# A fused attention and long-convolution kernel on one core: another prologue, and the order of the fill

## The chip, the cores and the metric

The kernel runs on one core of a Trainium2 chip. The metric is device time of one execution in microseconds (us), the median of several runs. A core has five engines that run their own instruction streams and meet at semaphores: TensorE (PE, matrix products into PSUM; its weight loads are counted apart as PEld), VectorE (DVE), ScalarE (ACT, here above all the exponential), GpSimd (POOL) and SyncE (SP, here only issuing DMAs). Several engines issue DMAs on queues of their own.

## What is computed

Two independent parts, side by side in the output of 2048 rows and 2 x 512 columns. Part A is attention with 32 heads of 16 columns that share one k and one v. Part B is a short causal convolution of k (4 taps) times v, then a causal convolution over all 2048 positions per channel, a skip term and a gate.

```python
q = (x @ wq).reshape(B, S, H, Dh).transpose(0, 2, 1, 3)      # S = 2048, D = 512, H = 32, Dh = 16
k, v = x @ wk, x @ wv                                        # one head of 16 for all
p = softmax(einsum("bhqd,bkd->bhqk", q, k) * Dh ** -0.5)
a = einsum("bhqk,bkd->bhqd", p, v).transpose(0, 2, 1, 3).reshape(B, S, D) @ wo

k_shift = sum(k_pad[:, t:t+S] * shift_k[:, 3-t] for t in range(4))
kv = k_shift * v
y = irfft(rfft(kv, 2S) * rfft(ssm_k, 2S))[:S] + kv * ssm_D
b = q * y
out = concatenate([a, b], axis=-1)
```

## The kernel before

**Attention in tiles.** Queries are cut in four quarters of 512, heads in groups of four; one such pair is a stack, 32 in all (`NQ`). A stack is 16 blocks of 128 keys times two, 32 tiles. A tile is: scores (`keys`, L937: eight products, 49 rows of the contraction) into one of two PSUM buffers, one exponential on ACT over 128x1024 (`exp`, L949), and products with v (`pv`, L973) that sum over the keys. The 49 rows are q's high part, its low part, one row with a bound on the score, and the high part again; so the exponential cannot overflow and no running maximum is needed. That row holds the norm bound |q| times max |k|, computed by PE from |q| and the maxima of k (`bound`, L709). High and low parts are two float16 tiles whose sum is the float32 value; a product of such numbers is three float16 products.

**Stacks go through DRAM.** Queries and bounds of four heads are written to the DRAM tile `qd`, and `stack` reads 49 rows per head back into the tile `st`. That puts the rows on the partitions on which the scores want them. Also the very first stack goes this way, except its bound row.

**The prologue** (`prologue`, `load`, `x_turn`) comes before the first tile. x arrives in four quarters of 1 MB. PE transposes each 128x128 block (L576), ACT makes the high part while it copies out of PSUM (L589), DVE the low part (L592). The first query group of the first quarter is multiplied out (L770, twelve products), clipped (L683), split and sent. Then k and v of all positions (`kv`, L601), their maxima over the positions (`km`, L610), the largest of them by head column (`k_max`, L645 to L651), k's rows in place (`kv_rows`, L617; `k_cut`, `k_rows`), the bound row (`first_bound`, `first_rows`, L722 and L729), and the first scores. Between these stand products on a tile of zeros whose result nobody reads (`warm`, L567).

**The fill.** `attend` writes the program tile by tile. Everything that is not scores, exponential and PV products is given by generator threads (`_Fill`): the other queries (`rest_of_q`), the convolution as Fourier transforms by products and butterflies (`conv_pe`, `conv_short`, `conv_dve`), the output projection (`wo_part`), the last keys of four stacks whose exponential DVE computes (`own`), and the way of x's quarters 2 and 3 to DRAM and back (`spill`). A thread yields how many products it wants, and a DVE cost; `turn` gives room on PE by the constants SLOT, SCORES, PV, UNIT and on DVE by a credit of RATE per tile. The order of the threads in `body` is their priority; `hurry` raises one that is near a due time. `after` holds a thread until another has set a mark. One PSUM buffer pair (tag f) of two holds the sums of PV, the other is left to the fill; each fill group starts when DVE has read the group before it.

Of the kernel before, what the change touches and what calls it, by code (L numbers as in the profile page):

```python
# [109 lines left out]
class _Emit:  # L110
# [75 lines left out]
    def dft16(self, c, first, second, sign):  # L186
# [39 lines left out]
        self.places = (f1, f2)  # L226
# [210 lines left out]
    def backward(self, blk, cx, places):  # L437
# [3 lines left out]
        g1, g2 = places  # L441
# [11 lines left out]
        yield WAIT, 5  # L453
# [21 lines left out]
    def conv_pe(self):  # L475
# [13 lines left out]
        yield from self.after(("y", 0))  # L489
        yield from self.backward(0, *self.sp["y", 0])  # L490
        yield from self.short(1)
        yield from self.after(("y", 1))
        yield from self.backward(1, *self.sp["y", 1])
# [23 lines left out]
    def conv_dve(self):  # L517
        nat = [0, 1, 2, 3]
        for blk, order in enumerate((("cx", "ch"), ("ch", "cx"))):
            for n in order:  # L520
                yield from self.after((n, blk))
                yield from self.dft16(self.sp[n, blk], nat, nat, -1)
            f1, f2 = self.places
            cx, ch = self.sp["cx", blk], self.sp["ch", blk]
            yield from self.product(cx, ch)
            self.seen.add(("p", blk))
            yield from self.dft16(cx, f2, f1, 1)
            self.sp["y", blk] = cx, self.places
            self.seen.add(("y", blk))


    def load(self):
# [6 lines left out]
        nc.scalar.dma_start(wkv[:, :, DH:32], I["A_wv"].rearrange("(k p) e -> p k e", p=P))  # L539
        self.msk = self.c.tile([P, 295], F32, name="msk")  # L540
        nc.scalar.dma_start(self.msk, I["msk"])
        xa = w.tile([P, 4, D], F32, tag="sp", bufs=1, name="xa")
# [5 lines left out]
        wqf = [w.tile([P, 4, P], F32, tag="s2", bufs=S2, name=self.nm("wqf")) for g in range(4)]  # L548
        self.wq = [w.tile([P, 2, 4, P], F16, tag="wq", bufs=4, name=self.nm("wq")) for g in range(4)]
        for c in range(4):  # L550
            for i in range(2):
                nc.sync.dma_start(self.xin[c][i], xr[c][:, 2 * i : 2 * i + 2, :])
            if c == 0:
                nc.sync.dma_start(wqf[0], wq[:, :, 0:P])
        for g in range(1, 4):
# [5 lines left out]
        self.parts(nc.gpsimd, self.wkv[:, 0], self.wkv[:, 1], wkv, WS)  # L561
        self.wqf = wqf
# [6 lines left out]
    def x_turn(self, c, b, between=lambda: None, cut=None):  # L569

        nc = self.nc

        def turn(dp, rows):
            for e in range(2):
                for i in rows:
                    nc.tensor.transpose(  # L576
                        b[dp][:, e, i * P : (i + 1) * P],
                        self.xin[c][i // 2][:, i % 2, (2 * dp + e) * P : (2 * dp + e + 1) * P],
                        self.ident,
                    )  # L580

        for rows in (range(2), range(2, 4)):
            for dp in range(2):
                turn(dp, rows)
            if rows.start == 0:
                between()
        for dp in range(2):
            hi, lo = (self.xT[c][:, i, 2 * dp : 2 * dp + 2, :] for i in range(2))
            nc.scalar.mul(hi, b[dp], XS)  # L589
            if cut is not None and dp == 0:  # L590
                self.q_hi(0, 0, cut)
            nc.vector.scalar_tensor_tensor(lo, b[dp], XS, hi, ALU.mult, ALU.subtract)  # L592
        if cut is not None:
            self.q_abs(0, 0, cut)

    def kv(self, b):

        order = [(i, j, dk) for dp in range(2) for i, j in ((0, 0), (1, 0), (0, 1)) for dk in (2 * dp, 2 * dp + 1)]
        for x in order:
            for c in range(4):  # L600
                self.nc.tensor.matmul(  # L601
                    b[32 * c : 32 * c + 32, :],
                    self.wkv[:, x[0], x[2], :],
                    self.xT[c][:, x[1], x[2], :],
                    start=x == order[0],
                    stop=x == order[-1],
                )
        kv = self.w.tile([P, 512], F32, tag="p", bufs=PB, name="kv")
        self.km = self.c.tile([P, 1], F32, name="km")
        self.nc.vector.tensor_reduce(self.km, b, AX.X, ALU.max, apply_absolute_value=True)  # L610
        self.nc.scalar.copy(kv, b)
        return kv

    def kv_rows(self, kv, c, b):

        r = slice(32 * c, 32 * c + 32)
        self.nc.tensor.matmul(b, self.msk[r, 163:291], kv[r, :], start=True, stop=True)  # L617

    def k_cut(self, b, a=0, n=512):
        cut = self.w.tile([P, n], F32, tag="s2", bufs=S2, name=self.nm("kc"))  # L620
        lim = lambda i: self.msk[:, 160 + i : 161 + i]
        self.nc.vector.tensor_scalar(cut, b[:, a : a + n], lim(0), lim(1), ALU.min, ALU.max)
        h16 = self.w.tile([P, n], F16, tag="gn", bufs=3, name=self.nm("kh"))
        return cut, h16

    def k_rows(self, c, cut, h16, a=0, n=512):

        ks = self.kst[:, c * 512 + a : c * 512 + a + n]
        self.nc.vector.scalar_tensor_tensor(ks, h16, self.msk[:, 162:163], cut, ALU.mult, ALU.add)

    def v_turn(self, kv, b):

        nc = self.nc
        for t in range(4):
            nc.tensor.transpose(b[:, t * P : (t + 1) * P], kv[:, t * P : (t + 1) * P], self.ident)
        bv = b.rearrange("p (t c m) -> p t c m", t=4, c=4)
        vx = self.vx.rearrange("p (c t) m -> p t c m", t=4)[:, :, :, 0:DH]
# [827 lines left out]
```

## Time and profile before

| what | value |
|---|---|
| median of three runs | 1005.63 us (1001.79 to 1005.63) |
| the profiled execution | 1004.58 us |
| its span, first to last instruction | 1002.3 us |
| mean granted TensorE clock | 0.993 |
| first exponential starts | 32.40 us |
| exponentials | 1016, busy 938.1 us |
| DMA | 83.12 MB |

The span is the time between the first and the last instruction in the trace; the execution's own time is taken from outside and 2.3 us longer. Busy time is the union of an engine's instructions, so 95% on ACT and 94% on PE do not say which of the two is the limit: that is read from what ended the idle time of each. The granted clock is the share of full speed that the throttle let TensorE have. A tile's row in the trace has the line of its helper, so all scores are L937 whatever the stack.

### The profile page before, as it was taken

What the parts mean: (1) busy time and instruction counts of PE and PEld (TensorE: products, weight loads), DVE (VectorE), ACT (ScalarE), POOL (GpSimd) and SP (SyncE); (2) the same over time, 40 slices, a digit from 0 to 9 for tenths busy, and PEclk for the clock granted to TensorE, in tenths of its full rate; (3) what the DMA queues carried; (4) which work ended last, traced back from release to release, by engine and by line L of the source; (5) the groups of instructions that cost most, each with busy time, mean ns of one, the idle gap of its engine ahead of it and who ended that gap; (6) DMA issues with size and microseconds to landing.
All of it is one profiled execution on the core that took longest, in us unless ns stands there. A gap on an engine that the chain in (4) does not pass through costs nothing.

```text
span 1002.3 us, 51255 instructions
## 1 busy us (share of the span) xinstructions
PE 940.9 (94%) x23463; PEld 459.4 (46%) x23463; DVE 746.3 (74%) x964; ACT 950.6 (95%) x1032; POOL 172.3 (17%) x305
## 2 busy tenths in 40 slices
PE   7999999999999999999989999999889989989996
PEld 4344444444544444444444544544334444444453
DVE  4637966888627988989888678599998827667753
ACT  4699999999999999999999999999999999999995
POOL 1542211410004000100054254000000033111000
PEclk9899999999999999999999999999999999999999
DMA  6262432423213211322143344111111133121101
GB/s 222 82 187 83 135 115 90 110 86 96 74 55 92 69 44 37 95 86 65 44 141 120 95 138 124 56 36 41 55 44 44 43 121 103 59 80 43 46 13 47
DMA packets 69461, 83.12 MB, mean 83 GB/s; under 512 B 20816, under 2 KB 58550, under 8 KB 69238
## 3 DMA queue, kind: packets, MB, share of 16 engines
q1 hardware_dynamic: 47430, 43.78, 13.8%
q0 software_dynamic: 20320, 35.46, 11.9%
q8 instruction: 185, 3.03, 1.3%
q10 hardware_dynamic: 1488, 0.54, 0.2%
q14 instruction: 38, 0.31, 0.1%
HBM read 54.66 MB, written 25.03 MB: 80 GB/s over the span
## 4 chain that ended last, share of the span: by engine, by line
PE 51%; ACT 26%; DVE 14%; issue 6%; DMA 2%; SPq 0%; POOL 0%; ACTq 0%; DVEq 0%; POOLq 0%
ACT p L949 26%; PE f L973 24%; PE s L937 14%; PE f L250 11%; DVE own L1036 3%; DVE sp L169 1%; DVE ao L982 1%; DMA xb<-in_A_x 1%; DVE ao L983 1%; DVE sp L290 1%; DVE sp L435 0%; PE f L617 0%; DMA qd<-qp 0%; DMA ff<-in_ff 0%; PE f L576 0%
## 5 line engine op out<-in xcount | busy, mean ns | idle before, releaser
L949 ACT ACTIVATE p<-s 128x1024 f32<-128x1024 f32 x1016 | 938.1, 1068 | 19.2 <-PE s L937 17.1
L973 PE MATMUL f<-p,vx 64*32 64x512 f32 (+1 forms) x8880 | 551.8, 554 | 2.2 <-DVE cut L683 1.1
L937 PE MATMUL s<-st,kst 49*32 49x512 f16 x8128 | 428.8, 381 | 33.2 <-ACT p L949 29.2
L937 PEld LDWEIGHTS <-kst 49*32 49x32 f16 x8192 | 200.2, 89 | 399.5 <-issue 353.2
L973 PEld LDWEIGHTS f<-p,vx 64*32 64x32 f32 x8880 | 175.4, 106 | 30.5 <-issue 3.7
L169 DVE TENSOR_TENSOR sp<-sp 128x1024 f32<-128x1024 f32 x96 | 111.1, 1215 | 0.0
L290 DVE COPY sp<-f 128x1024 f32<-128x1024 f32 x32 | 39.1, 1223 | 64.1 <-PE f L250 64.1
L295 POOL DMA_DIRECT2D ff<-in_ff x64 | 34.5, 545 | 277.8 <-ACT p L949 276.1
L982 DVE COPY ao<-f 128x512 f32<-128x512 f32 (+1 forms) x33 | 22.2, 674 | 55.2 <-PE f L973 55.1
L250 PE MATMUL f<-wo,o 64*32 64x512 f16 x1440 | 57.0, 375 | 1.7 <-DVE cut L683 0.9
L169 DVE TENSOR_TENSOR sp<-sp,sp 128x1024 f32<-128x1024 f32 x48 | 56.1, 1217 | 0.3
L250 PE MATMUL f<-xT,wq 64*32 64x512 f16 x1344 | 53.4, 375 | 1.8 <-DVE gm L733 1.2
L295 POOL DMA_DIRECT2D fi<-in_fi x32 | 17.8, 560 | 180.3 <-ACT p L949 180.3
L250 PE MATMUL f<-a,ff 64*32 64x256 f32 x1024 | 42.4, 378 | 1.1 <-DVE a L407 0.6
L250 PE MATMUL f<-hT,ff 64*32 64x256 f32 x1024 | 40.8, 377 | 1.3 <-DVE sp L290 1.2
L467 DVE TENSOR_TENSOR r<-f,q 128x512 f32<-128x512 f32 x16 | 11.0, 689 | 41.2 <-PE f L250 41.2
L250 PE MATMUL f<-sp,fi 64*32 64x256 f32 x1024 | 40.4, 376 | 0.9 <-DVE r L467 0.9
L469 POOL DMA_DIRECT2D out<-r x32 | 17.8, 560 | 124.7 <-DVE r L467 114.1
L405 DVE TENSOR_TENSOR a<-a,t 128x512 f32<-128x512 f32 x48 | 33.2, 692 | 1.6
L396 DVE TENSOR_TENSOR t<-kk,tpb 128x512 f32<-128x512 f32 (+1 forms) x50 | 33.0, 663 | 0.9 <-DMA qd<-qp 0.9
L323 POOL DMA_DIRECT2D hin<-in_B_ssm_k x32 | 21.1, 665 | 64.5 <-ACT p L949 63.1
L250 PEld LDWEIGHTS <-o 64*32 64x32 f16 x1440 | 22.6, 93 | 16.2 <-DVE cut L683 1.8
(166 smaller groups left out, 732.3 us busy)
## 6 DMA issues: line engine op xcount, KB each, us to landing
ff<-in_ff POOLq DMA_DIRECT2D x64, 128.0 KB, 2.9
od<-ao SPq DMA_DIRECT2D x60, 128.0 KB
qd<-qp SPq DMA_DIRECT2D x48, 128.0 KB
st<-qd SPq DMA_DIRECT2D x62, 98.0 KB
kk<-in_B_k POOLq DMA_DIRECT2D x32, 128.0 KB, 2.8
v<-in_B_v POOLq DMA_DIRECT2D x32, 128.0 KB, 3.4
hin<-in_B_ssm_k POOLq DMA_DIRECT2D x32, 128.0 KB, 5.5
fi<-in_fi POOLq DMA_DIRECT2D x32, 128.0 KB, 3.3
```

Of the source, the lines that this page charges most:

```text
L169: v.tensor_tensor(part(out), part(a), part(b), op)
L250: y = self.nc.tensor.matmul(out[j : j + 32, cols], w[r, j : j + 32], x[r], start=half == m == 0, stop=half == 1 and m == k - 1,)
L290: self.nc.vector.tensor_copy(out, self.both.rearrange("p i (q n) -> p i q n", q=2))
L295: self.paced(self.nc.gpsimd.dma_start(t[:, i], self.I[n][:, 2 * m2 + i]))
L323: self.paced(nc.gpsimd.dma_start(dst, src))
L396: nc.vector.tensor_tensor(out[:, n], kk[:, x], tap(i, n.stop - n.start), ALU.mult)
L405: nc.vector.tensor_tensor(a, a, t, ALU.add)
L937: self.nc.tensor.matmul(s[j : j + 32, e, :], self.kst[rows, k * P + j : k * P + j + 32], self.st[n][rows, a, cols], start=True, stop=True,)
L949: self.exps[u % 4] = self.nc.scalar.activation(self.pt[u], s, AF.Exp, scale=LN2 * DH**-0.5 / SC / SC)
L973: nc.tensor.matmul(self.acc[e][32 * j : 32 * j + 32, m], vx[rows, :], y, start=k == 0, stop=stop)
L982: nc.vector.tensor_copy(a, self.acc[0][:, m])
L1036: v.scalar_tensor_tensor(g, g if i < 4 else y, c[i], y if i else x.bitcast(BF16), ALU.add, ALU.mult)
```

## The change

**Prologue.** x's transposes, high parts and low parts are cut in pieces (`x_turn`, `x_hi`, `x_lo`) and written out in one list, with the twelve query products in between and no products on zeros but the first ten. The low part of x's last quarter isn't made there: ACT copies the transposed values from PSUM to the tile `xa`, and fill makes it later. The first stack's query rows are put in place on chip: `sel`, a matrix of zeros and ones made by POOL from the identity, is multiplied with the split queries, and the bound is summed into the same PSUM by the weights `wbn`. The bound uses a maximum of k that comes from the product of the high parts alone (`kv_max`), with -1.02 for the scale. k's first 512 columns come in two halves from weights `wkx` that hold wk at the row places (`k_first`). The high parts of three query weights stay on POOL, the low parts go to DVE, as fill. v's weights are loaded on SP's queue and split later.

**First stack.** Exact k and v (`kv`), the other k rows in halves of 256 (`k_chunk`), v's transposes (`v_turn`), the missing low part, the exact maximum and a check that the first bound held (into `gm`) are the start of `rest_of_q`. The PV products of the first stack start at tile 7 in place of 3, by a table in `plan`; its first four exponentials go to a buffer of their own.

**Later stacks.** The queries of the second quarter wait for the transforms of the first channel half (`cx`, `ch`), those of the last quarter for `cx` of the second; the inverse transform's thread starts its loads at a mark `soon`, 28 steps into the last butterflies, in place of at their end; the third stack's load is issued at tile 22 of the second. The last store's second half is issued by ACT in place of SP.

On ACT in the prologue, from the conversions of the third quarter of x to the first exponential. Names: `xT` high parts of x, `wq` query weights, `qp` and `qa` split and absolute queries. Before:

```order
L589 ACTIVATE xT<-x_168 128x1024
L589 ACTIVATE xT<-f_192 128x1024
L589 ACTIVATE xT<-f_228 128x1024
L672 CAST qp_247<-cut_226 128x512
L589 ACTIVATE xT<-x_229 128x1024
L678 ACTIVATE qa_253<-cut_226 128x512
L611 COPY kv<-x_272 128x512
L786 CAST kh_337<-kc_335 128x256
L638 ACTIVATE vx<-x_325 128x4x4x16
L949 ACTIVATE p_365<-s_356 128x1024
```

After:

```order
L606 ACTIVATE xT<-x_211 128x1024
L606 ACTIVATE xT<-f_234 128x1024
L606 ACTIVATE xT<-f_244 128x1024
L606 ACTIVATE xT<-x_245 128x1024
L816 COPY xa<-f_244 128x1024
L818 ACTIVATE qa_299<-cut_225 128x512
L835 COPY xa<-x_245 128x1024
L837 CAST st_301<-f_302 128x512
L1056 ACTIVATE pfirst<-s_329 128x1024
```

The conversions follow each other without the query's split between them; the copy of k and v, a cast and v's scaling are gone, and two copies of x and half of the first stack's tile have come.

On DVE, from the last low parts to the rows ahead of the first scores and behind. Before:

```order
L592 SCALAR_TENSOR_TENSOR xT<-f_228,xT 128x1024
L592 SCALAR_TENSOR_TENSOR xT<-x_229,xT 128x1024
L610 TENSOR_REDUCE km<-x_272 128x1
L645 TENSOR_SCALAR kx<-msk,km 128x4
L622 TENSOR_SCALAR kc_335<-f_328,msk 128x256
L650 TENSOR_REDUCE kmr<-x_325 128x1
L651 TENSOR_SCALAR wb<-msk,kmr 128x8
L629 SCALAR_TENSOR_TENSOR kst<-kh_337,msk,kc_335 128x256
L729 TENSOR_SCALAR st_267<-f_342 1x512 x4
```

After:

```order
L610 SCALAR_TENSOR_TENSOR xT<-f_234,xT 128x1024
L815 TENSOR_REDUCE ks<-x_266 128x1
L649 TENSOR_SCALAR ks<-msk,ks 128x4
L664 TENSOR_SCALAR kc_307<-f_267,msk 128x256
L653 TENSOR_REDUCE ks<-x_266 128x1
L831 TENSOR_SCALAR wbn<-msk,ks 128x4
L671 CAST kh_315<-kc_307 128x256
L673 SCALAR_TENSOR_TENSOR kst<-kh_315,msk,kc_307 128x256
L836 CAST st_301<-f_302 128x512
```

The last quarter's two low parts no longer stand ahead of the reduction; four one-row writes of the bound have become one copy of the whole tile (and one on ACT).

On PE in the first stack, between the scores of the tiles 15 and 16, after the change. `f_377` is the fill's PSUM pair, `kv` the exact k and v, `msk` the placing matrix:

```order
L1039 MATMUL s_655<-st_301,kst 32x512
L638 LDWEIGHTS wkv
L638 MATMUL f_377<-xT,wkv 32x512
L658 MATMUL f_377<-kv,msk 128x256
L1039 LDWEIGHTS kst
L1039 MATMUL s_674<-st_301,kst 32x512
```

Before, the placing product of a later chunk stood two tiles ahead of need, and over the whole 512 columns:

```order
L937 MATMUL s_395<-st_267,kst 32x512
L617 MATMUL f_406<-kv,msk 128x512
L937 LDWEIGHTS kst
L937 MATMUL s_420<-st_267,kst 32x512
L937 LDWEIGHTS kst
```

What moved is that the scores of tile 16 now read the half chunk whose product stands directly ahead of them.

```diff
-            f1, f2 = self.places
+            f1, f2 = self.place
...
-            yield from self.dft16(cx, f2, f1, 1)
-            self.sp["y", blk] = cx, self.places
+            for i, x in enumerate(self.dft16(cx, f2, f1, 1)):
+                if i == 28:
+                    self.seen.add(("soon", blk))
+                yield x
+            self.sp["y", blk] = cx, self.place
...
+    def places(self):
...
+        for i in range(2):
+            for r in (0, DH, BR + 1):
+                for e in range(2):
+                    nc.gpsimd.tensor_scalar(
+                        self.wkx[:, i, :, 64 * e + r : 64 * e + r + DH], self.wkv[:, i, :, 0:DH], 1.0, None, ALU.mult
+                    )
+        x = self.ident[:, 0:64].rearrange("p (a e d) -> p a e d", a=2, e=2)
+        for i, r in ((0, 0), (1, DH), (0, BR + 1)):
+            y = self.sel[:, :, i, :].rearrange("p a (e r) -> p a e r", e=2)[:, :, :, r : r + DH]
+            nc.gpsimd.tensor_scalar(y, x, 1.0, None, ALU.mult)
...
+    def kv_max(self, b, c, dks):
+
+        for dk in dks:
+            for i in c:
+                self.nc.tensor.matmul(
+                    b[32 * i : 32 * i + 32], self.wkv[:, 0, dk, :], self.xT[i][:, 0, dk, :], start=dk == 0, stop=dk == 3
+                )
...
+    def k_chunk(self, c, b, h):
+
+        r, a = slice(32 * c, 32 * c + 32), CB * h
+        self.nc.tensor.matmul(b[:, a : a + CB], self.msk[r, 163:291], self.kvt[r, a : a + CB], start=True, stop=True)
+        self.k_split(c, self.k_cut(b[:, a : a + CB]), h)
...
+    def k_split(self, c, cut, h):
...
+        v.tensor_copy(h16, cut)
+        ks = self.kst[:, c * 512 + CB * h : c * 512 + CB * h + CB]
+        v.scalar_tensor_tensor(ks, h16, lim(2), cut, ALU.mult, ALU.add)
...
-        warm(far[1], 4)
-        far += [self.wide()]
-        self.x_turn(1, far, lambda: warm(far[2], 3))
...
+        self.x_q(0, 0, (0, 1), q)
+        self.x_q(0, 0, (2, 3), q)
+        self.x_q(1, 0, (0, 1), q)
+        for dp in both:
+            T(1, dp, 0, t1[dp])
+        self.x_q(1, 0, (2, 3), q)
+        for dp in both:
+            T(1, dp, 1, t1[dp])
+            hi(1, dp, t1[dp])
+        lo(1, 0, t1[0])
+        t2 = [self.wide()]
+        for i in both:
+            T(2, 0, i, t2[0])
+        hi(2, 0, t2[0])
+        self.x_q(0, 1, range(4), q)
+        cut = self.q_cut(q)
...
+        lo(1, 1, t1[1])
+        t2 += [self.pair()]
+        for i in both:
+            T(2, 1, i, t2[1])
+        hi(2, 1, t2[1])
+        t3 = [self.pair(), self.wide()]
+        for dp in both:
+            for i in both:
+                T(3, dp, i, t3[dp])
+            hi(3, dp, t3[dp])
...
+        self.kv_max(kh, range(4), (0, 1))
+        self.kv_max(kh, range(3), (2, 3))
+        self.k_first(kb, 0, range(4))
+        self.kv_max(kh, (3,), (2, 3))
+        self.k_first(kb, 0, range(4, 12))
...
+            nc.tensor.matmul(b[:, 0, :], self.sel[:, 0, i, :], qp[:, i, :], start=i == 0, stop=False)
...
+        for a in both:
+            nc.tensor.matmul(b[:, a, :], self.wbn[:, a, :], qa, start=False, stop=True)
+        self.k_split(0, kc, 0)
+        nc.scalar.copy(self.xa[:, 2:4], t3[1])
+        nc.vector.tensor_copy(st[:, 0, :], b[:, 0, :])
+        nc.scalar.copy(st[:, 1, :], b[:, 1, :])
...
+                if c == 1:
+                    yield from self.after((("ch" if g else "cx"), 0))
+                if c == 3:
+                    yield from self.after(("cx", 1))
...
+        first = {0: (7,), 4: (8,), 2: (9, 11), 24: (25, 27), 28: (29,)}
+        first.update({x: (x + 4 if x < 26 else 28,) for x in (*range(6, 24, 2), 26)})
...
-            if t - self.base[n] == (6 if n else 22) and n + 1 < NQ:
+            if t - self.base[n] == (6 if n > 1 else 22) and n + 1 < NQ:
...
-            nc.sync.dma_start(xr[3][:, 3, h], y[3][:, h])
+            (nc.scalar if h.start else nc.sync).dma_start(xr[3][:, 3, h], y[3][:, h])
```

356 lines of the change are left out of this document (201 added, 155 removed).

## The prediction

> **What bounds the kernel now.** I read first the page's busy times, then the groups of instructions by line for ScalarE (ACT) in two stretches, then the waits of ACT, and last the timeline of the first 45 us.
>
> ```profile
> span 1002.3 us, 51255 instructions
> PE 940.9 (94%) x23463; PEld 459.4 (46%) x23463; DVE 746.3 (74%) x964; ACT 950.6 (95%) x1032; POOL 172.3 (17%) x305
> ...
> L949 ACT ACTIVATE p<-s 128x1024 f32<-128x1024 f32 x33 | 31.4, 1037 | 4.5 <-PE s L937 4.0 <-ACT p L949 0.4
> ...
> L949 ACT ACTIVATE p<-s 128x1024 f32<-128x1024 f32 x984 | 907.8, 1069 | 14.7 <-PE s L937 13.2 <-ACT p L949 0.3
> ...
> ACT p L949 <- PE s L937: 17.1, 20, 1.9
> ```
>
> The third line is the window from 32 to 67 us (the first stack of 32 tiles and one more), the fourth the rest up to 988 us. The 1016 exponentials run back to back at 907.8/984 = 0.92 us each; nothing in this change makes one cheaper or drops one. So the time splits into four pieces: what passes before the first exponential, the stops in the first stack (4.5 us), the stops in all later stacks (14.7 us), and the end after the last exponential. The waits say what a stop is: scores that PE delivers late, 20 times, 1.9 us at worst. I price the change on these four pieces.
>
> **The start, before.** These rows are the path to the first exponential: start, duration, engine, line.
>
> ```profile
> 10.74 1.12 PE L576 MATMUL f<-ident,xb 128*128 128x128 f32 x8 [1.95 <-DMA xb<-in_A_x]
> 12.93 1.91 PE L576 MATMUL f<-ident,xb 128*128 128x128 f32 x8
> 14.03 1.94 ACT L589 ACTIVATE xT<-f 128x1024 f16<-128x1024 f32 x2 [4.04 <-PE f L576]
> 17.73 2.75 PE L770 MATMUL x<-xT,wq 128*128 128x512 f16 x12
> 23.26 1.03 ACT L589 ACTIVATE xT<-x 128x1024 f16<-128x1024 f32 x1
> 23.45 1.16 POOL L673 TENSOR_TENSOR qp<-cut,qp 128x512 f16<-128x512 f32 x1 [12.95 <-ACT qp L672]
> 24.17 2.02 PE L601 MATMUL x<-xT,wkv 128*32 128x512 f16 x29 [0.21 <-DVE xT L592]
> 24.32 1.23 DVE L592 SCALAR_TENSOR_TENSOR xT<-x,xT 128x1024 f16<-128x1024 f32 x1 [0.21 <-ACT xT L589]
> 24.69 1.49 POOL L273 TENSOR_SCALAR wq<-wqf 128x512 f16<-128x512 f32 x1
> 26.23 0.69 DVE L610 TENSOR_REDUCE km<-x 128x1 f32<-128x512 f32 x1 [0.68 <-PE x L601]
> 26.95 0.23 DVE L645 TENSOR_SCALAR kx<-msk,km 128x4 f32<-128x4 f32 x1
> 27.59 1.12 PE L617 MATMUL f<-kv,msk 32*128 32x512 f32 x2 [0.86 <-ACT kv L611]
> 28.64 0.39 PE L646 MATMUL x<-kx,msk 128*128 128x4 f32 x2
> 28.75 0.55 DVE L622 TENSOR_SCALAR kc<-f,msk 128x256 f32<-128x256 f32 x1 [1.57 <-PE f L617]
> 29.38 0.40 ACT L786 CAST kh<-kc 128x256 f16<-128x256 f32 x1 [1.84 <-DVE kc L622]
> 29.52 0.16 DVE L650 TENSOR_REDUCE kmr<-x 128x1 f32<-128x4 f32 x1 [0.22 <-PE x L567]
> 29.79 0.23 DVE L651 TENSOR_SCALAR wb<-msk,kmr 128x8 bf16<-128x8 f32 x1
> 29.92 0.48 DVE L629 SCALAR_TENSOR_TENSOR kst<-kh,msk,kc 128x256 f16<-128x256 f16 x1
> 30.49 1.41 DVE L729 TENSOR_SCALAR st<-f 1x512 f16<-1x512 f32 x2
> 31.57 0.78 PE L937 MATMUL s<-st,kst 49*32 49x512 f16 x8
> 32.40 1.02 ACT L949 ACTIVATE p<-s 128x1024 f32<-128x1024 f32 x1 [0.28 <-PE s L937]
> ```
>
> Three things are to be seen. The last high part of x is ready only at 23.26 + 1.03 = 24.29, since the twelve query products (17.73, 2.75 us) stand on PE ahead of the last quarter's transposes. Then the bound waits for the low parts too (DVE to 25.55, then products), so its reduction starts at 26.23. And from there 6.17 us pass to the first exponential.
>
> **The start, after.** (1) The twelve products are spread in groups of two and four between the transposes. ACT then has six high-part conversions of 0.97 (1.94/2) behind each other from 14.03: they could end at 19.9 if none waited. One waits: the sixth transpose group takes the buffer of the query products and so stands behind the clip on DVE, where a low part is ahead of it; I put 1.1 us there, one conversion. That gives 21.0 in place of 24.29. Bounds: 19.9, and 24.3 if the new order wins nothing. (2) The bound's reduction needs high parts alone: two products of 512 columns, 2 x 2.75/12 = 0.46, so it starts at about 21.5 in place of 26.23. (3) From there DVE and PE alternate: 0.69 + 0.23 + 0.39 + 0.16 + 0.23 = 1.70, two products with the bound's weights 0.46 (PE), meanwhile on DVE the cast (at most ACT's 0.40) and the 0.48 of kst, then the copy of the finished 128x512 query tile out of PSUM. Its price is the clip's, below, 0.68. Then 0.83 from scores to exponential (31.57 to 32.40), and some 0.05 to 0.1 at each of eight handovers, as between 29.75 (0.23 from 29.52) and 29.79 and the like: 0.5. Sum 1.70 + 0.88 + 0.68 + 0.83 + 0.5 = 4.6, in place of 6.17. The first exponential starts at 26.1; with the bounds of (1), 25.0 to 29.4. I take **-6.2 us**.
>
> ```profile
> 20.82 0.68 DVE L683 TENSOR_SCALAR cut<-x 128x512 f32<-128x512 f32 x1
> ...
> 7.85 0.54 POOL L273 TENSOR_SCALAR wkv<-wkvf 128x128 f16<-128x128 f32 x1 [6.99 <-DMA wkvf<-in_A_wv]
> ...
> 9.50 0.52 POOL L749 MEMSET vx<- 128x512 f32 x1
> ...
> 10.29 0.20 POOL L662 TENSOR_SCALAR wb<-msk 128x8 bf16<-128x8 f32 x1
> ...
> 27.36 2.12 SPq L893 DMA_DIRECT2D st<-qd  x4
> ```
>
> What else the change puts there costs nothing as far as these rows show. POOL builds the placed weights with three clears and fifteen copies of 64 elements a partition. No row has that size; between 0.20 (8 elements) and 0.54 (128) I take 0.3, since 64 lies midway: 15 x 0.3 + 3 x 0.5 (the clear of vx) = 6 us, begun near 8, over by 15; the clip needs POOL only after 16. Then the split of the queries (1.49 + 1.16) and v's weights (3 x 0.3) end near 20, ahead of the bound's first product. If POOL ran twice as long, it would be 4 us late and eat most of the gain. On SP the four loads of the first stack (2.12 us at 27.36, with a wait for the queries' own writes) leave the path: the tile is made on chip. Their writes to DRAM go out behind it; the second stack reads them some 30 us later. The load of v's weights moves to SP ahead of three weight loads that nobody needs before 20.
>
> **The first stack.** Exact k, v and rows become fill. The stops of before and the pieces of the new chain:
>
> ```profile
> 34.60 3.98 ACT L949 ACTIVATE p<-s 128x1024 f32<-128x1024 f32 x4 [1.19 <-PE s L937]
> ...
> 34.72 0.37 DVE L800 CAST kh<-kc 128x256 f16<-128x256 f32 x1
> 35.12 0.79 DVE L629 SCALAR_TENSOR_TENSOR kst<-kh,msk,kc 128x256 f16<-128x256 f16 x1
> ...
> 39.85 1.02 ACT L949 ACTIVATE p<-s 128x1024 f32<-128x1024 f32 x1 [1.27 <-PE s L937]
> ...
> 42.09 1.02 ACT L949 ACTIVATE p<-s 128x1024 f32<-128x1024 f32 x1 [1.22 <-PE s L937]
> ```
>
> Before, three stops of 1.2 us. After, each half of a later chunk of k passes PE and DVE: a product of 256 columns (1.12/2 = 0.56), clip 0.55, cast 0.37, kst 0.48 to 0.79, then scores 0.78: 2.7 to 3.1 us. For tiles 16, 20 and 24 the order has the product behind the scores of the tile just ahead, which leaves two exponentials, 1.84 us: 0.9 to 1.2 late, three times. For tile 8 there are two more, but DVE has the low parts of three query weights (3 x 0.68) and a copy of kv ahead: 0.4 late. Queued behind these waits on PE is every later score and the PV products; ACT waits for the scores. Together 3.7 in place of 4.5: **-0.8 us** (-3 if DVE is never late, +4 if each of the six halves costs the longest 1.2 us and the clock falls as below).
>
> **Later stacks.** The moved fill is the same work in another sequence: the queries of the second quarter wait for the convolution's transforms, and the inverse transform's tables load on POOL (17% busy) before its input is ready. A stop there is one start of a fill group behind a DVE read of its PSUM buffer; the number of such starts stays. So 14.7 us stays: **0**, bounded by -4 and +5, a quarter and a third of it.
>
> **The end.** The last store moves from SP to ACT's queue.
>
> ```profile
> 995.18 0.37 ACTq L1231 DMA_DIRECT2D out<-y  x1
> 995.40 1.97 SPq L1235 DMA_DIRECT2D out<-y  x2
> ```
>
> Two issues behind each other on SP took 1.97; one on ACT's queue takes 0.37 and can run beside the first. **-0.8 us**, between 0 and -1.5.
>
> Sum: -6.2 - 0.8 + 0 - 0.8 = -7.8. The profiled execution took 1004.58 (its span 1002.3 and 2.3 around it); 1004.6 - 7.8 = **997** us. The median of the three runs shown, 1005.63, lies 1 us above it.
>
> [...] The old prologue had fourteen products on zeros between its steps; the new one keeps only the first ten. The granted clock of before (the column ahead of the DMA share):
>
> ```profile
> 12.00:14.00 2.00, 2.00 (x9) 1.44 (x7) 0.00 (x0) 0.00 (x0) 0.00 (x0) 0.50 1.01 412
> ...
> 36.00:40.00 4.00, 3.97 (x35) 1.02 (x42) 3.90 (x5) 2.63 (x4) 2.67 (x4) 0.50 0.39 131
> ```
>
> At half clock eight transposes took 1.91 against 1.12. [...] I leave the sum.
>
> **The rivals.** *The gain is given back.* The start comes to 29.4 (PE at half clock through the transposes, or POOL late) and the halves of k cost 1.2 six times, 7.2 in place of 4.5: -3.0 + 2.7 - 0.8 = -1.1, 1003.5. For it: the half clock at 36 to 40, just where the little products of the first stack stand. Against it: half of each chunk has two exponentials more than it needs. *The convolution's fill makes DVE late.* With queries of the second quarter held until the transforms are through, PE fill groups meet a DVE that still has butterflies queued. Price: if the 13.2 us of later stops double, -7.8 + 13.2, 1010; it ends slower than before by more than the bound from some 12.8 us of extra stops, that is fifteen more of the mean 17.1/20 = 0.86. Against it: the DVE is 74% busy and the fill is not more. *The conversions are no earlier*, all else as forecast: 1000.
>
> **How the numbers follow.** About 0.5% (5 us) is what a measurement of this kernel can tell from no change. My forecast, around 997 with 992 to 1000.5 as its own range, has 0.60; conversions no earlier 0.10, half of it on either side of the bound; the gain given back 0.18; late DVE 0.12, nearly all slower. So faster 0.64, same 0.25, slower 0.11. The range leaves out most of the last case and takes in the second: 990 to 1005.
>
> **What would show it.** Right: the first exponential at 25 to 28 us; the reduction that opens the bound near 21.5; stops of about 1 us ahead of exponentials 16, 20 and 24 and none of 1.2 before tile 8; 13 to 16 us of stops later. Wrong: a gap on ACT between the conversions of the third quarter of x; POOL's query split ending after 21; a granted clock of 0.50 over the whole first stack; or later stops above 20 us, which would make the prediction wrong by themselves.

## The result, and the profile after

The changed kernel took 1008.63 us, the median of 20 runs, against 1004.90 for 20 runs of the kernel before: a ratio of 1.0036 with a 95% interval of 1.0022 to 1.0049. That is 0.36% slower, inside the 0.5% that counts as no change, and outside the range of 990 to 1005. The profiled execution took 1009.57 us. Cut at four instants, the spans of the two profiles compare so:

| piece (us) | before | after | difference | forecast |
|---|---|---|---|---|
| span's start to first exponential | 32.40 | 25.55 | -6.8 | -6.2 |
| exponential 0 to 32, the first stack | 34.58 | 44.08 | +9.5 | -0.8 |
| exponential 32 to 1015, later stacks | 921.4 | 923.4 | +2.0 | 0 |
| last exponential's end to span's end | 12.92 | 13.65 | +0.7 | -0.8 |

The gain at the start came, and the first stack gave it back with interest. These are ACT's exponentials of the first stack in the timeline of after (start, duration, operation; at the end the idle time ahead and what ended it):

```profile
25.55 3.90 ACT L1056 ACTIVATE pfirst<-s 128x1024 f32<-128x1024 f32 x4
29.53 3.03 ACT L1056 ACTIVATE p<-s 128x1024 f32<-128x1024 f32 x3
32.99 1.02 ACT L1056 ACTIVATE p<-s 128x1024 f32<-128x1024 f32 x1 [0.43 <-PE s L1039]
34.54 1.02 ACT L1056 ACTIVATE p<-s 128x1024 f32<-128x1024 f32 x1 [0.53 <-PE s L1039]
35.92 1.02 ACT L1056 ACTIVATE p<-s 128x1024 f32<-128x1024 f32 x1 [0.35 <-DVE kc L664]
38.00 1.04 ACT L1056 ACTIVATE p<-s 128x1024 f32<-128x1024 f32 x1 [1.06 <-PE s L1039]
39.36 4.69 ACT L1056 ACTIVATE p<-s 128x1024 f32<-128x1024 f32 x5 [0.33 <-PE s L1039]
45.81 4.05 ACT L1056 ACTIVATE p<-s 128x1024 f32<-128x1024 f32 x4 [1.76 <-PE s L1039]
51.69 1.02 ACT L1056 ACTIVATE p<-s 128x1024 f32<-128x1024 f32 x1 [1.82 <-PE s L1039]
53.35 2.14 ACT L1056 ACTIVATE p<-s 128x1024 f32<-128x1024 f32 x2 [0.64 <-PE s L1039]
56.10 1.02 ACT L1056 ACTIVATE p<-s 128x1024 f32<-128x1024 f32 x1 [0.61 <-PE s L1039]
59.01 1.02 ACT L1056 ACTIVATE p<-s 128x1024 f32<-128x1024 f32 x1 [1.89 <-PE s L1039]
60.52 1.02 ACT L1056 ACTIVATE p<-s 128x1024 f32<-128x1024 f32 x1 [0.48 <-PE s L1039]
62.25 1.02 ACT L1056 ACTIVATE p<-s 128x1024 f32<-128x1024 f32 x1 [0.71 <-PE s L1039]
64.39 1.02 ACT L1056 ACTIVATE p<-s 128x1024 f32<-128x1024 f32 x1 [1.11 <-PE s L1039]
```

The three large stops stand ahead of exponentials 16, 20 and 24 (45.81, 51.69 and 59.01), where the forecast put stops of 0.9 to 1.2. They are 5.5 us together. Around them are smaller ones, for which the forecast had 0.4 us; with them ACT stands idle for 12.4 us in the first stack, where the forecast had 3.7. The windows of the same profile show their company; after the window stand its length, the busy times of PE, weight load, DVE, ACT and POOL, the granted clock, the DMA share and GB/s:

```profile
31.40:34.80 3.40, 2.29 (x32) 1.17 (x24) 2.02 (x5) 2.44 (x4) 0.00 (x0) 1.00 0.35 116
34.80:38.20 3.40, 3.40 (x42) 1.11 (x48) 2.78 (x5) 1.99 (x3) 0.00 (x0) 0.50 0.34 114
48.40:51.90 3.50, 2.01 (x43) 0.79 (x35) 2.02 (x4) 1.67 (x3) 2.40 (x4) 1.00 0.16 46
51.90:55.30 3.40, 3.40 (x49) 0.68 (x39) 1.49 (x3) 2.67 (x3) 1.66 (x3) 0.50 0.26 70
55.30:58.70 3.40, 2.26 (x38) 0.93 (x30) 2.83 (x7) 1.22 (x2) 1.08 (x2) 1.00 0.56 103
58.70:65.50 6.80, 6.80 (x90) 2.49 (x82) 2.21 (x6) 4.10 (x4) 2.67 (x5) 0.50 0.68 201
```

Each of these three stretches in which PE waits (busy 2.0 to 2.3 of 3.4) is followed by a stretch at half clock in which PE is busy throughout and ACT is not (one more, 41.7 to 45.1 with PE busy 2.13 of 3.41, is followed by full clock): 2.67 of 3.40 behind exponential 20, 4.10 of 6.80 behind exponential 24. So two things could carry the 9.5 us: the late halves of k themselves, and the half clock. One late half, for tile 16, in the timeline:

```profile
42.43 0.41 PE L1039 MATMUL s<-st,kst 49*32 49x512 f16 x8
42.77 0.39 PE L638 MATMUL f<-xT,wkv 128*32 128x512 f16 x1
43.09 0.69 PE L658 MATMUL f<-kv,msk 32*128 32x256 f32 x2
43.83 0.54 DVE L664 TENSOR_SCALAR kc<-f,msk 128x256 f32<-128x256 f32 x1 [2.92 <-PE f L658]
44.40 0.29 DVE L671 CAST kh<-kc 128x256 f16<-128x256 f32 x1
44.73 0.48 DVE L673 SCALAR_TENSOR_TENSOR kst<-kh,msk,kc 128x256 f16<-128x256 f16 x1
45.27 0.41 PE L1039 MATMUL s<-st,kst 49*32 49x512 f16 x8 [1.49 <-DVE kst L673]
```

From the product (43.09) to the exponential (45.81) pass 2.72 us. The exponential ahead ends at 45.81 - 1.76 = 44.05, so 0.96 us of this is covered, one exponential, and PE idles 1.49 us. (The x2 in the L658 row is one product of 256 columns in f32, recorded in two parts.)

### The profile page after: what moved, and what is told of

Its sections match the earlier page's. It is cut to its first block, busy times and chain, and to the rows that moved or that the text cites. A ratio compares the mean times of both kernels' runs of the same rounds, so it can differ in the third digit from the quotient of the medians.

```text
span 1007.7 us, 51389 instructions
## 1 busy us (share of the span) xinstructions
PE 945.7 (94%) x23517; PEld 460.7 (46%) x23517; DVE 751.1 (75%) x985; ACT 952.5 (95%) x1031; POOL 173.2 (17%) x320
## 3 DMA queue, kind: packets, MB, share of 16 engines
q1 hardware_dynamic: 47558, 43.48, 13.6%
## 4 chain that ended last, share of the span: by engine, by line
PE 49%; ACT 30%; DVE 12%; issue 7%; POOL 1%; DMA 1%; ACTq 0%; DVEq 0%
ACT p L1056 30%; PE f L1080 24%; PE s L1039 14%; PE f L250 10%; DVE own L1148 2%; DVE sp L169 2%; DVE ao L1089 1%; DVE ao L1090 1%; DMA wkvf<-in_A_wk 1%; DVE sp L290 1%; DVE sp L435 0%; PE f L638 0%; DVE sp L219 0%; PE f L658 0%; DVE u L218 0%
## 5 line engine op out<-in xcount | busy, mean ns | idle before, releaser
L1039 PEld LDWEIGHTS <-kst 49*32 49x32 f16 x8192 | 197.5, 90 | 402.1 <-issue 350.5
L250 PE MATMUL f<-xT,wq 64*32 64x512 f16 x1344 | 51.9, 375 | 0.0
```

Of the source, the lines that this page charges most:

```text
L250: y = self.nc.tensor.matmul(out[j : j + 32, cols], w[r, j : j + 32], x[r], start=half == m == 0, stop=half == 1 and m == k - 1,)
L1039: self.nc.tensor.matmul(s[j : j + 32, e, :], self.kst[rows, k * P + j : k * P + j + 32], self.st[n][rows, a, cols], start=True, stop=True,)
```

## The experiments

Theory A: the late halves carry the loss. Theory B: the half clock does, and it comes from how little of PE's array is in use. Theory C: the new sequence in later stacks carries its 2.0 us. Theory D: the store on ACT's queue carries the 0.7 at the end. Each ratio is to the kernel before on the same chip, with its 95% interval. The profiles are cut at the same instants as above; each cut is of one execution, so that a difference in them counts here only where the medians of the runs bear it out:

| kernel | median us | ratio | first exponential | exponential 0 to 32 | 32 to 1015 | end |
|---|---|---|---|---|---|---|
| early_k | 1004.0 | 0.998 [0.996, 1.000] | 25.9 | 40.8 | 921.3 | 13.2 |
| warm_fill | 1006.4 | 1.001 [0.999, 1.003] | 25.6 | 43.8 | 920.8 | 13.1 |
| old_store | 1009.5 | 1.004 [1.002, 1.006] | 26.1 | 44.4 | 923.6 | 13.1 |
| no_soon | 1009.4 | 1.005 [1.003, 1.007] | 25.5 | 44.2 | 922.4 | 13.4 |
| early_k4 | 998.8 | 0.993 [0.990, 0.996] | 25.6 | 35.1 | 921.6 | 13.6 |
| hold4 | 1000.2 | 0.995 [0.992, 0.997] | 25.4 | 37.5 | 922.3 | 13.2 |
| hold | 1004.8 | 1.000 [0.998, 1.002] | 26.1 | 41.2 | 921.8 | 13.0 |
| early_six | 997.2 | 0.991 [0.989, 0.993] | 25.9 | 33.7 | 921.7 | 13.1 |
| six | 1006.0 | 1.001 [1.000, 1.003] | 26.1 | 44.7 | 924.2 | 13.6 |

### The last store and the inverse transform

```diff
# old_store
-            (nc.scalar if h.start else nc.sync).dma_start(xr[3][:, 3, h], y[3][:, h])
+            nc.sync.dma_start(xr[3][:, 3, h], y[3][:, h])
# no_soon
-        yield WAIT, 4
-        yield from self.after(("y", blk))
+        yield WAIT, 5
...
-        yield from self.after(("soon", 0))
+        yield from self.after(("y", 0))
         yield from self.backward(0)
...
-        yield from self.after(("soon", 1))
+        yield from self.after(("y", 1))
```

> The changed kernel with the last store of the output back on SP's queue, nothing else. My prediction's step (the store ends the run, worth 0.8): last exponential to the end 13.65 grows to 14.4, total 1009.4. Theory D (the 0.7 that the end grew by came with the store on ACT's queue): 12.9, total 1007.9. If the store ends nothing: 13.65 within 0.1, 1008.6.

> The changed kernel with the inverse transform started when its input is whole, as before the change, and with its first wait of 5, nothing else. Theory C (the new sequence in later stacks carries the 2.0 us that exponential 32 to 1015 grew by): 921.4 in place of 923.4, total 1006.6. Rival (those 2.0 are stray stops and half clock, as much as two executions of one kernel differ by): 923 within 2, total 1008.6.

Both come out beside after (1.0036): 1.0037 and 1.0053, with intervals that overlap its own. The end is 13.1 us with the store on SP, between after's 13.65 and before's 12.92, and it is 13.0 to 13.7 in the nine profiles that have the store on ACT's queue: neither my step (it ends the run) nor D is shown, and the 0.7 lies within what one code varies by. From the end of the last exponential to the last group of products 4.0 us pass in before, after and old_store alike, so what differs lies behind that. Later stacks took 922.4 us in no_soon, and 920.8 to 924.2 over all ten profiles other than before's; theory C has nothing to explain that two executions would not. The gates that hold the queries of the second and fourth quarter back, and the start of the third stack's loads at slot 22, were not tried alone.

### Halves earlier, clock held at the stops

```diff
# early_k: chunk 2's halves come behind scores 10 and 15, chunk 3's behind 22 and 25
+        yield WAIT, 1
+        yield 0, 1500
+        self.k_chunk(2, kvb[:, 1, :], 0)
         for dp in range(2):
...
-        self.k_chunk(2, kvb[:, 1, :], 0)
-        yield WAIT, 0.5, CONT
-        n = 9
+        self.k_chunk(2, kvb[:, 1, :], 1)
+        n = 8
...
-        self.k_chunk(2, kvb[:, 1, :], 1)
# warm_fill, in scores()
+        if u in (16, 20, 24):
+            self.warm(s[:, 0, :], self.xT[0][:, 0, 0, :], 5)
         return self.keys(s, n, k, a, cols)
```

> The changed kernel with the four halves of the last two chunks of k (product, clip, cast, kst) issued two to six score tiles ahead of the tile that reads them, in place of one; the last part of kv, the exact bound and the turn of v stand behind them. Nothing is left out. Theory A (the late halves carry the loss): the stops of 1.76, 1.82 and 1.89 us ahead of exponentials 16, 20 and 24 go, 5.5 us; if the stretches at half clock behind them (52 to 55 and 58.6 to 65.4 us) go too, another 4.9. First exponential unchanged at 25.6, exponential 0 to 32 in 34 to 39 us in place of 44.1, total 998 to 1003. Theory B (the half clock is its own cause, it comes with the many little products whatever their place): stops go, half clock stays, 1003. Rival (PE and DVE simply have too much work in the first stack): the stops move to other tiles, 44 us stay, 1008.

> The changed kernel with five products of 128x128 on 512 columns (some 0.22 us each) written into the score tile ahead of scores 16, 20 and 24, where PE idles 1.49 us; the scores overwrite them. Theory B (PE's idle time at the stops brings the half clock): the clock stays at 1.00 from 50 to 66 us, the excess of exponentials 20 to 29 over 0.92 that is no stop (4.9 us) goes, and 16, 20 and 24 still stop 1.8 us: exponential 0 to 32 in 39 us, total 1003.7. Theory A alone (the stops are the cost, the clock follows from something else): the half clock stays, 44 us, 1008.6 or up to 1 us more where the products delay the scores.

early_k kept one stop of 1.55 us ahead of exponential 16, by another wait: the next product of kv writes the PSUM tile that the clip reads, so it queued behind DVE ahead of the scores.

```profile
45.87 0.38 PE L638 MATMUL f<-xT,wkv 128*32 128x512 f16 x1 [1.29 <-DVE kc L664]
46.17 0.41 PE L1037 MATMUL s<-st,kst 49*32 49x512 f16 x8
...
46.72 1.02 ACT L1054 ACTIVATE p<-s 128x1024 f32<-128x1024 f32 x1 [1.55 <-PE s L1037]
```

Half clock stayed at 35.6 to 39.0 and 56.1 to 62.9. So A held for the stops it could take, but the first stack took 40.8 us in place of 34 to 39, and B's "stops go, clock stays" was not tested cleanly either, since one stop stayed. In warm_fill the clock stayed at 1.00 behind exponentials 16 and 20, as B said, but fell ahead of exponential 24 (57.9 to 61.3) and for two windows at 34.0. The stops ahead of 16 and 20 stayed (1.72 and 1.81), and the one ahead of 24 grew to 4.70: its five unread products ran at half clock and took 2.31 us on the way to the scores. The first stack still took 43.8, near A's 44, but the median of 1006.4 is neither B's 1003.7 nor A's 1008.6.

### What the clock goes by

The clock's rows in these six profiles (before, after and the four above) showed a pattern that I had not expected. Every change lies on a grid of 3.413 us (in before the long stretch at full clock, from 42.4 to 998.1, is 955.73 us, 280 steps of 3.4133; the distances between changes in one profile are whole multiples of that step to within 0.04, the last stretch before the program ends excepted), whose offset to the program's start differs between executions. So I added up, for each interval of that grid, rows x columns of the weights x streamed columns over all PE records, f32 counted four times, scaled so that one product of 128x128 on 512 columns in f16 stands for 0.213 us of full use (close to their spacing in the trace, where four take 1.03 us and two 0.60: 0.43/2 = 0.215). This is a measure of mine, and the weight of f32 in it a choice that no run isolates. PE's busy time alone separates the intervals worse: in before, between 9 and 985 us, the one interval at full clock that half clock followed (32.1 to 35.5) had PE busy for 3.28 of its 3.41 us, and 89 of the 281 others no longer; by the use, 0.32, it is the lowest of them all. The use can exceed 1, since products overlap (the eight of one tile's scores take 0.41 us together, 0.38 each by their own records) and f32 may be over-counted. Some intervals, with the clock that was granted in them:

```
start  use  clock      start  use  clock      start  use  clock
after                  early_k4               early_six
 28.0  0.62  1.0        28.6  0.54  1.0        27.7  0.70  1.0
 31.4  0.33  1.0        32.0  0.42  1.0        31.1  0.72  1.0
 34.8  0.78  0.5        35.5  0.95  0.5        34.5  1.20  1.0
 38.2  1.55  1.0        38.9  1.06  1.0        37.9  1.05  1.0
 41.7  0.61  1.0        42.3  1.31  1.0        41.3  1.35  1.0
 45.1  1.19  1.0        45.7  0.96  1.0        44.7  0.97  1.0
 48.5  0.39  1.0        49.1  1.17  1.0        48.1  1.13  1.0
 51.9  0.74  0.5        52.5  1.30  1.0        51.6  1.35  1.0
 55.3  0.43  1.0        55.9  1.61  1.0        55.0  1.59  1.0
 58.7  0.60  0.5        59.3  1.28  1.0        58.4  1.24  1.0
 62.1  0.87  0.5        62.8  0.96  1.0        61.8  0.99  1.0
```

Over all eleven profiles, between 9 and 985 us, 3105 intervals ran at full clock, and 32 of them were followed by half clock. All 15 below 0.40 were, 22 of 25 below 0.50, one of 3017 above 0.65. In between it is open: of the 63 from 0.50 to 0.65 nine fell. Of 41 at half clock 33 returned, most at 0.64 or more (one at 0.45), and eight at 0.24 to 0.63 did not. Much of what is open there comes from the weight given to f32. With f32 counted twice in place of four times, a weight chosen only after all these traces were there, over the same intervals, all 32 that were followed by half clock lie at 0.36 or below, and only 4 of the other 3073 do (counted four times, 57 of those lie no higher than the highest that fell; counted once, 10). By the same count the 33 that returned to full clock lie at 0.38 or above, and the eight that did not at 0.35 or below.

This is a regularity of these traces, not a mechanism that a run isolates; the runs that follow were built on it, with f32 counted four times. The 3.413 and 0.65 that theory B names in what I expected of them are read off such intervals; it is a theory there, and of the 63 between 0.50 and 0.65 only nine fell.

### Each little product in its own slot; unread products

```diff
# early_k4, against the changed kernel (order in rest_of_q)
+        self.k_chunk(2, kvb[:, 1, :], 0)
+        self.x_lo(3, 0, self.xa[:, 0:2])
+        yield WAIT, 0.5
+        self.k_chunk(2, kvb[:, 1, :], 1)
+        self.x_lo(3, 1, self.xa[:, 2:4])
...
+        self.k_chunk(3, kvb[:, 1, :], 0)
+        yield WAIT, 0.5, CONT
...
-        self.k_chunk(3, kvb[:, 1, :], 0)
# hold4, hold: in scores(); the first counts are hold4's, the second hold's
+        self.warm(s[:, 0, :], self.xT[0][:, 0, 0, :], {16: 2, 18: 1, 20: 2, 21: 1, 22: 1, 23: 1, 24: 2, 25: 1, 26: 1}.get(u, 0))
+        self.warm(s[:, 0, :], self.xT[0][:, 0, 0, :], {16: 5, 20: 5, 21: 1, 22: 1, 23: 2, 24: 5, 25: 2, 26: 2}.get(u, 0))
# hold4, hold, early_six, six: in rest_of_q
+        vb = self.bank()
+        self.warm(vb, self.xT[0][:, 0, 0, :], 3)
         self.k_chunk(1, kvb[:, 1, :], 0)
         yield 3, 400, CONT, 3
-        self.v_turn(slice(0, 96), self.bank())
+        self.warm(vb, self.xT[0][:, 0, 0, :], 3)
+        self.v_turn(slice(0, 96), vb)
```

In early_k4 chunk 2's halves come behind scores 10 and 12, chunk 3's behind 19 and 25 (in the changed kernel behind 15, 19, 23 and 25); `yield` lines that only set costs are left out.

> As early_k, with each of the little products (halves of k, last part of kv, exact bound, turn of v) in a slot of its own, so that none stands on PE directly behind a DVE read of the same PSUM buffer; chunk 2 is two tiles earlier still. Nothing is left out. Theory A (the late halves carry the loss): the last stops, 1.7 us ahead of exponential 16 and the two near 22 and 23 (0.7 and 0.9), go; exponential 0 to 32 in 34 to 36 us, total 1000. Theory B (the grid: the clock is set anew every 3.413 us by how much of the array the window used; windows with less than about 0.65 fall): the window before 35 us (0.39 in early_k) is untouched, so one stretch of 3.4 us at half clock stays there, and another near 55 in most executions; total 1001 to 1003, and the runs still spread over 8 us or more with their mean clock.

> early_k4 with 18 products of 128x128 on 512 columns that nobody reads: six around the first half of chunk 1, in PSUM columns that the turn of v uses later, and twelve in the score tiles 16 to 26, each overwritten by the scores. Theory B: each adds 0.213/3.413 = 0.06 to its window's use of the array, the clock stays at 1.00 from the first exponential to 70 us, exponential 0 to 32 in 32 to 34 us, total 995 to 998, and the spread over runs falls to some 5 us. Theory A alone: the products only take PE's time, 18 x 0.22 = 4.0 us at most on the path, total 1002 to 1005.

> The changed kernel with 24 such products: six around the first half of chunk 1 and 18 in the score tiles 16 and 20 to 26 (five each in 16, 20 and 24, where PE idles 1.49 us); the halves of k stay where the change put them. Theory B: the clock stays at 1.00 through the first stack, the three stops of 1.8 us stay, exponential 0 to 32 in 36 to 38 us in place of 44.1, total 1000. Theory A: with the halves still late the stops and what follows them stay, 42 to 45 us, total 1007 to 1010.

ACT's exponentials in early_k4:

```profile
34.63 2.04 ACT L1057 ACTIVATE p<-s 128x1024 f32<-128x1024 f32 x2 [0.53 <-PE s L1040]
37.66 1.02 ACT L1057 ACTIVATE p<-s 128x1024 f32<-128x1024 f32 x1 [0.99 <-PE s L1040]
40.25 1.94 ACT L1057 ACTIVATE p<-s 128x1024 f32<-128x1024 f32 x2 [1.57 <-PE s L1040]
42.73 19.96 ACT L1057 ACTIVATE p<-s 128x1024 f32<-128x1024 f32 x21 [0.55 <-PE s L1040]
```

From 42.73 on 21 exponentials run without a stop: the stops at 16, 20 and 24 are gone, and with them the half clock behind them. The first stack took 35.1 us, A's number, though nothing was done for the clock there. The median, 998.8, is 9.8 us below after's. What is left is the half clock at 35.5 to 38.9, as B said, with stops of 0.99 and 1.57 in and behind it; and the seven runs spread over 8.1 us, as B said too.

hold and hold4 kept the clock at 1.00 through the whole first stack, B's first claim. But hold4's first stack is longer than early_k4's (37.5 against 35.1; B had 32 to 34): the likely reason is that each unread product in a score tile takes PE's time ahead of the scores. The medians, 1000.2 and 998.8, are too close to tell apart; hold4's spread did fall, to 2.8 us. And in hold the three stops stayed, one grew:

```profile
35.32 7.87 ACT L1060 ACTIVATE p<-s 128x1024 f32<-128x1024 f32 x8 [0.53 <-PE s L1043]
44.95 4.05 ACT L1060 ACTIVATE p<-s 128x1024 f32<-128x1024 f32 x4 [1.76 <-PE s L1043]
50.82 1.02 ACT L1060 ACTIVATE p<-s 128x1024 f32<-128x1024 f32 x1 [1.82 <-PE s L1043]
...
58.60 1.02 ACT L1060 ACTIVATE p<-s 128x1024 f32<-128x1024 f32 x1 [2.52 <-PE s L1043]
```

At full clock the late halves cost what they cost in after. Neither theory had hold's numbers (41.2 us and 1004.8): A said 42 to 45 and 1007 to 1010, B 36 to 38 and 1000. So B alone falls, and A alone too: holding the clock won 2.9 us of the first stack (44.1 to 41.2, net of the products' own price; 3.9 in the medians), moving the halves 9.0 (44.1 to 35.1), and that takes in the half clock that went with the stops.

### Six unread products alone

> early_k4 with only the six unread products around the first half of chunk 1 (three behind scores 6, three behind scores 7), where PE waits 0.45 and 0.67 us. Theory B: the window before 35 us rises from 0.42 to 0.6 or above (0.60 in hold4, where the clock stayed), exponential 0 to 32 in 33.3 us in place of 35.1, total 997 and a smaller spread. Rival (the price is again PE's time, as with the twelve later products of hold4): 35 us, total 999 to 1000.

> The changed kernel with only these six products. Theory B with A: the half clock at 34.8 to 38.2 goes (some 2 us of exponentials 8 to 11), the three late halves and the half clock after them stay, exponential 0 to 32 in 42 us in place of 44.1, total 1006.5. Rival (they only shift the stops): 44 us, 1008.6.

early_six has the lowest median of the study: 997.2 us, ratio 0.9913 [0.9893, 0.9933]. It is faster than before and after; against early_k4 (0.9928 [0.9898, 0.9957]) the two intervals overlap, and early_k4 has the shortest single run (993.6). The first stack took 33.7 us; B had 33.3, the rival 35. The six products lift the interval at 31.1 to 0.72, and the clock stays at 1.00 to 66 us, beyond the end of the first stack at 59.6. Windows and exponentials of its profile:

```profile
31.00:34.50 3.50, 3.50 (x34) 1.39 (x28) 1.89 (x4) 2.84 (x3) 0.00 (x0) 1.00 0.37 120
34.50:52.00 17.50, 17.44 (x331) 6.68 (x330) 12.08 (x24) 15.49 (x17) 0.50 (x1) 1.00 0.27 86
...
35.15 3.06 ACT L1060 ACTIVATE p<-s 128x1024 f32<-128x1024 f32 x3 [0.53 <-PE s L1043]
39.08 1.94 ACT L1060 ACTIVATE p<-s 128x1024 f32<-128x1024 f32 x2 [0.87 <-PE s L1043]
41.57 20.88 ACT L1060 ACTIVATE p<-s 128x1024 f32<-128x1024 f32 x22 [0.54 <-PE s L1043]
```

Its six runs lie within 2.6 us (995.5 to 998.1), where the seven of early_k4 spread over 8.1 and the 16 of before on the same chip over 6.3. So the smaller spread is what these runs show of the six products; a gain in the median they do not show beyond the noise.

six has a median of 1006.0, near the 1006.5 expected, but its profile is of the longest of the twelve executions (1009.6 us of span). There the half clock at 34.8 was gone, as in hold, and exponential 16 came at 44.97 in place of 45.81, but then the clock fell at 45.4, 52.2 and 59.1, four intervals in all, as many as in after, and the first stack took 44.7. The rival's 44 fits that one profile, B's 1006.5 the median; six and after are not clear of each other (1.0013 [0.9995, 1.0031] against 1.0036 [1.0022, 1.0049]).

## Why the prediction was wrong, point by point

**The start** (-6.2, first exponential at 26.1; 32.40 - 26.1 is 6.3) came out right: 25.55. In part that was luck, since two errors cancelled. The high parts were through at 19.2, 1.8 earlier than the 21.0 I put. But between them and the reduction I had put two products, 0.46 us, and 2.1 passed: the bound's products first waited 0.98 us for POOL's split of v's weights, and four products of k's first columns stood ahead of their last two. So the reduction started at 21.26, against 21.5 forecast.

```profile
18.16 1.02 ACT L606 ACTIVATE xT<-x 128x1024 f16<-128x1024 f32 x1
...
19.10 1.04 PE L630 MATMUL x<-xT,wkv 128*32 128x512 f16 x14 [0.98 <-POOL wkv L273]
20.07 0.61 PE L624 MATMUL f<-xT,wkx 128*128 128x256 f16 x4
20.61 0.60 PE L630 MATMUL x<-xT,wkv 128*32 128x512 f16 x2
...
21.26 0.69 DVE L815 TENSOR_REDUCE ks<-x 128x1 f32<-128x512 f32 x1 [2.08 <-PE x L630]
```

The tail of the chain took 4.29 (25.55 - 21.26) against 4.6.

**The first stack** (-0.8, bounds -3 and +4) is the step that failed; it measured +9.5. The length of a late half's chain was right (2.72 of "2.7 to 3.1"). Its stops were put at 3.7 us, 3.3 in three large ones and 0.4 ahead of tile 8, and measured 12.4: 5.5 in the three, 6.9 in smaller ones. So the smaller stops are the larger part of the miss. Of the steps behind these numbers three were wrong:

- "which leaves two exponentials, 1.84 us": the cover was 0.96. Scores of a tile wait for the buffer of the tile two ahead, so the product behind scores 15 can begin only after exponential 13 ends (it is the third of the five in the row at 39.36, and scores 15 start at 42.43); with a product of kv ahead of it, exponential 14 was nearly over (43.09, while exponential 15 ended at 44.05). Three stops of 1.76 to 1.89 in place of 0.9 to 1.2: 1.9 to 2.8 us more than forecast. They are 5.5 us in all, and hold shows that they stand at full clock too.
- The half clock was put at the far bound with the case that every half costs the longest 1.2. It came behind the stops of 1.8 that only three had. What it costs: early_six takes 33.7 us with neither; after takes 44.1, 10.4 more; 5.5 of these are the three stops, and the other 4.9 bound what the half clock can cost, in four intervals of 3.4 us. Holding the clock by unread products recovered 2.9 net of their own price. In hold, at full clock, the smaller stops are still 3.7 us, against 6.9 in after; so about half of them goes with the half clock. For the rest of them no run isolates a cause.
- The same half clock went with the interval before 35 us, where PE has little to do until v is turned (busy 2.29 of 3.40 us in after); early_six against early_k4 prices it at 1.4 us of the first stack (35.1 to 33.7), in one profile of each; the 1.6 in the medians is not clear of their noise.

**Later stacks** (0, -4 to +5): 2.0 more in this pair of profiles. Over the ten profiles of the new order this piece varied from 920.8 to 924.2, about before's 921.4, and after's extra goes with two intervals at half clock there (133.8 and 256.7), where before had none. The step stands within its bounds.

**The end** (-0.8): not seen. +0.7 in the profile, nothing between old_store and after in the medians. What ends the program there is not settled.

**The filler left out.** I left the sum as it was, with nothing in it for half clock. Where I looked, in the prologue, that was right: with the filler between the steps gone the granted clock was 1.00 from 4.1 to 34.8 us of after, and the 0.50 of before at 11.6 to 15.0 did not come. Where I did not look, in the first stack, it fell for four intervals of 3.4 us. The intervals ahead were not idle ones (PE busy 2.0 to 2.3 of 3.4); by the measure above the use was 0.33, 0.39 and 0.43 ahead of the first three, and 0.60 in the third, at half clock itself, ahead of the fourth. The prediction's row of before at 36 to 40 has half clock beside PE busy for 3.97 of 4.00 us in that same stretch; by the counts above that half clock goes with the interval ahead, 32.1 to 35.5, where the use was 0.22 with f32 counted twice.

**The rivals.** *The gain is given back* (1003.5) came nearest. Its second half, the late halves and the half clock of the first stack, is what happened, 6.8 us dearer than its 2.7 more; its first half did not happen, for the start was kept whole (-6.8 in place of its -3.0). *The convolution's fill makes DVE late* did not happen: later stops (14.7 before) are 16.6. *The conversions are no earlier* did not happen. Of the marks under "what would show it", the first two held, none of 1.2 stood before tile 8 (0.53 there, 0.4 forecast), and later stops were 16.6 where 13 to 16 were to show; the stops at 16, 20 and 24 were in the right place at nearly twice the size; the clock was at 0.50 over a third of the first stack, where I had asked for all of it.

With the halves earlier and in slots of their own (998.8) the changed kernel comes within 2 us of the forecast (997). Its first stack took 35.1 us, where the forecast's -0.8 makes 33.8 and had counted 3.7 us of stops in it.

## What to carry to other kernels

When a short chain through another engine feeds the next tile, count its cover from the moment at which the product can really start (here the buffer two tiles ahead, and what else stands in front of it in the queue), not from the number of tiles in between; three halves issued four to seven tiles earlier made 9 us here, together with slots of their own for the products. Look, for a stall on PE, not only at how long it is but also at the granted clock of the stretch behind it: here half clock came behind the stops, and holding the clock won 2.9 us net of the products' own price, beside 5.5 of stops. Unread products cost where they stand ahead of scores (twelve more of them: 3.8 us of the first stack and 3.0 of the median between early_six and hold4). Where PE waits anyway, six of them held the clock and narrowed the spread of the runs; their 1.6 us in the median are not clear of noise.

## What was unexpected in the hardware

The granted clock changed only on a grid of 3.413 us, fixed within an execution and shifted between executions, in all eleven profiles. In these profiles half clock came behind intervals of low use by the measure above, and PE's busy time does not single them out as well (3.28 of 3.41 us in the one of before): with f32 counted twice, all 32 intervals that were followed by 0.50 lie at 0.36 or below, and 4 of the other 3073. What makes the clock fall no run isolates. Execution times go with the clock: over the 20 runs of after the mean granted clock (0.984 to 0.994) and the time correlate at -0.89, 0.92 us for each 0.001. old_store and after have the same code in the first stack and had the half clock at other places (50.2 and 57.0 to 67.3, against 34.8, 51.9 and 58.7), with the grid shifted by 1.7 us against the program's start; that the shift is the cause was not tested.
